# Head of an attention and feed-forward kernel: first loads re-dealt over three queues, q and half of v held until S1 lands, and PE filler matmuls laid differently

## The chip, the cores and the metric

The kernel runs on one core of a Trainium2 chip. Its metric is the time of one execution on the device in microseconds, the median of six runs. Five engines work side by side: PE (matrix products), DVE (VectorE), ACT (ScalarE), POOL (GpSimd) and SP (SyncE, which only issues transfers). Each runs its own list of instructions in order and meets the others through semaphores.

## The reference, cut to what matters

```python
batch, n_heads, seq, head_dim, r = 4, 4, 1088, 32, 8      # q, k, v: (4, 4, 1088, 32); S1, S2: (8, 32)

def phi(x):                       # polynomial sketch: 64 features from two 8-wide sketches
    a = np.einsum('rd,bhsd->bhsr', S1, x)
    b = np.einsum('rd,bhsd->bhsr', S2, x)
    return np.einsum('bhsi,bhsj->bhsij', a, b).reshape(*x.shape[:-1], r * r)
q_p, k_p = phi(q), phi(k)
kv = np.einsum('bhsf,bhsd->bhfd', k_p, v)
z = np.sum(k_p, axis=2)
attn = np.einsum('bhsf,bhfd->bhsd', q_p, kv) / (np.einsum('bhsf,bhf->bhs', q_p, z)[..., None] + 1e-06)
x = attn.transpose(0, 2, 1, 3).reshape(4352, 128)
h = x @ moe_w_in                  # (4352, 2048)
out = (h - np.tanh(h)) @ moe_w_out
```

## The kernel before

**Stages.** For each batch the kernel loads k, v and q with tokens on partitions, transposes k (`kT`), sketches it on PE (`ksk`), transposes the sketch back on DVE (`kab`), forms its outer products on DVE (`w`), and multiplies them with v on PE (`kvmm`, L740). The result is spread over a block pattern (`kvd` on ACT, `kvt` on PE, `kvb` on ACT). A Gram matrix of the k sketch (`gram`, L672; `gm`, L678; `scmm`, L682) gives the sum over tokens that the denominator needs. q is transposed (`qT`, L594), sketched, divided (`m`, `den`, `rd`, `ap`) and expanded (`qp`, `qpT`), and PE forms the attention output (L846), which ACT writes to `xT`. The feed-forward part runs over ten groups of 192 to 512 tokens: 16 products with w_in (L959), tanh on ACT (L964), 16 products with w_out (L974), a transposing copy on DVE (L983) and stores. h itself goes into the output through w_in times w_out, formed once on PE (L918, L930; `wch`, `wcl`).

**Order.** Nothing is written out in engine order. Each operation is added with what it reads and writes, a key, and an estimate of its time. `_Prog.schedule` then places operations one by one, the earliest that can start first, keys deciding among near ones, with an estimate for the landing of each load. `_Prog.sync` sets the semaphore waits. So an edit of an estimate can change an engine's order; on the chip each engine then runs its fixed list and waits for what really happens.

**The head, batch 0.** It is split finer than the other batches. k comes in two parts (`KPARTS`: blocks 0 to 3 and 4 to 8), each as two loads, one of 192 or 240 KB on SP and one of 64 or 48 KB on ACT. The two sketch matrices S1 and S2 go to `sq` as two loads of 16 KB; DVE transposes them (`stt`, L541) and forms `wab` (L549), the weights of the k sketch; POOL forms `s2r` (L559) and part of `wq3` (L544), the weights of the q sketch. The rest of `wq3` (`sc0`, L695) needs `scmm`. For the first two blocks of q, `q_tok` (L646) multiplies the transposed q with `wq3`, and the other seven blocks follow after `kvt`.

**Loads.** All go through `load` (L463), in the order of their keys, each on the queue of the engine given to it. Before, SP issues k's first big part, S1, k's second big part, q's first 128 KB, and two quarters of v; ACT issues S2, k's two small parts, the other two quarters of v, and the rest of q (416 KB). Then follow, on SP, four quarters of w_in (256 KB each), and on POOL two halves of w_out (`wo`). A limit on the bytes in flight (`IN_FLIGHT`) makes later loads wait for earlier ones. ACT casts w_in to bf16 as it comes (L912, eight casts `wi`).

**Fillers.** Where the planner sees PE idle for longer than a threshold and the first output bank isn't used yet, `fill` inserts matmuls of a zero tile `zz` (L426, 128x128x128 bf16), whose result nobody reads. Their number is fixed when the program is built. `WARM` is the time up to which the planner counts PE operations double.

Of the kernel before, what the change touches and what calls it, by code (L numbers as in the profile page):

```python
# [17 lines left out]

GCOLS = [256, 384, 448] + [512] * 6 + [192]
T_FIRST = 12500.0  # L20
KPARTS = [(0, 4), (4, 9)]
IN_FLIGHT = [4000000, 1600000, 1600000, 900000]
WIDE = 7
# [57 lines left out]

class _Op:
    __slots__ = ("engs", "fn", "key", "deps", "users", "nleft", "vals", "eng", "lat", "mode",
                 "t0", "t1", "seq", "known", "waits", "inc", "cnt", "sem", "dma", "name", "filler")


class _Prog:
    SWITCH = 95.0
    WARM = 9000.0

    def __init__(self):
        self.ops = []
# [2 lines left out]
    def add(self, engs, fn, r=(), w=(), key=0.0, chain=None, dma=0, name="", after=(), mode=None):  # L95
        o = _Op()
        o.engs = engs
        o.fn, o.key, o.dma, o.name, o.mode = fn, key, dma, name, mode
        o.deps, o.users, o.vals = {}, [], []
        o.filler = False  # L100
        tag = next(iter(o.engs)) if len(o.engs) == 1 and not dma else None
        for kind, vs in (("r", r), ("w", w)):
            for v in vs:
                if v not in o.vals:
                    o.vals.append(v)
                    v.left += 1
                ph = v.phases
                same = ph and ph[-1][0] == kind
                if same and v.psum and (tag is None or ph[-1][1] != tag):
                    same = False  # L110
                if not same:
                    ph.append((kind, tag, []))
                if len(ph) > 1:
                    raw = kind == "r" and ph[-2][0] == "w"
                    for d in ph[-2][2]:
                        o.deps[d] = o.deps.get(d, False) or raw
                if kind == "r":
                    for p in reversed(ph[:-1]):
                        if p[0] == "w":
                            for d in p[2]:  # L120
                                o.deps[d] = True
                            break
                ph[-1][2].append(o)
        for d in after:
            o.deps.setdefault(d, False)
        if chain is not None:
            o.deps.setdefault(chain, False)
        o.deps.pop(o, None)
        self.ops.append(o)
        return o  # L130

    def schedule(self, filler=None):
# [6 lines left out]
        free = {"tensor": 1100.0, "vector": 900.0, "scalar": 900.0, "gpsimd": 900.0, "sync": 800.0}  # L139
        self.order = {e: [] for e in free}  # L140
        dma_free = 0.0
# [21 lines left out]
        while n < len(self.ops):  # L163
            best = None
            for e in free:
                cands = []
                for o in ready:
                    if e in o.engs:
                        t = start_of(o, e)
# [4 lines left out]
                t0, f = min(cands, key=lambda x: (x[0], x[1].key))  # L174
# [6 lines left out]
            _, t, o, e = best  # L181
# [11 lines left out]
                    for d in v.first_deps:  # L193
                        o.deps.setdefault(d, False)
            if e == "tensor":
                if filler is not None and t - free[e] > 150.0 and not filler[2].used:
                    self.fill(filler, free[e], t)
                if pemode is not None and o.mode != pemode:
                    t += self.SWITCH
                pemode = o.mode  # L200
# [4 lines left out]
            if o.dma:  # L205
                free[e] = t + occ
                st = max(t + 1400.0, dma_free)
                dma_free = st + o.dma
                o.t1 = dma_free + (1200.0 if o.key < -95000 else 700.0 if o.key < -89950 else 1500.0)
            else:  # L210
                o.t1 = t + occ
                free[e] = o.t1
# [21 lines left out]
    def fill(self, filler, a, b):  # L234
        t = a
        while True:
            cold = 2.0 if t < self.WARM else 1.0
            occ = 54.0 * cold
            if t + occ + 60.0 > b:
                break  # L240
            o = _Op()
            o.engs = {"tensor": (occ, 215.0)}
            o.fn, o.key, o.dma, o.name, o.mode = filler[0], 0, 0, "fill", "128x128"
            o.deps, o.users, o.vals = {filler[1]: True}, [], []
            o.filler = True
            o.eng, o.t0, o.t1, o.lat = "tensor", t, t + occ, 215.0
            o.inc, o.sem, o.waits, o.known = False, None, [], {}
            o.seq = len(self.order["tensor"])
            self.order["tensor"].append(o)
            t = o.t1  # L250

    def sync(self, nc):
        known = {e: {} for e in self.order}
# [79 lines left out]
def bass_polysketch_attn__then__act_tanh_shrink_kernel(  # L333
# [74 lines left out]
    sq = sb("sq", [128, 2, 32])  # L408
# [46 lines left out]
    for b in range(B):  # L455
        P.add(_v(256), lambda e, n, b=b: e.memset(vL[b][96:128, :, 224:288], 0.0), w=[vvals[b][3]], key=-89000 + b)

    def load(key, o_, i_, w, nbytes, eng="sync", rate=320.0):
        need, j = nbytes, len(flight)
        while j > 0 and need + flight[j - 1][1] <= limit[0]:  # L460
            j -= 1
            need += flight[j][1]
        o = P.add({eng: (1100.0 if eng == "gpsimd" else 450.0, 0.0)}, lambda e, n: e.dma_start(out=o_, in_=i_), w=w, key=key, dma=nbytes / rate,  # L463
                  after=[f[0] for f in flight[:j]])
        flight.append((o, nbytes))
        return o

    flight, limit = [], [IN_FLIGHT[0]]

    def load_s(key, x, Sx, eng):  # L470
        load(key, sq[:, x, :], Sx[None, :, :].to_broadcast([16, 8, 32]), [sqv], 16384, eng)

    kpad = _Val(ap=kL[0][:, 1088:1152])
    pool_op(lambda e, n: e.memset(kpad.ap, 0.0), w=[kpad], n=64, key=-49500)
# [6 lines left out]
    def load_k(key, b):  # L481
        src = k[b].rearrange("h (t c) d -> (h t) (c d)", c=NC)
        if b == 0:
            kd = kL[b].rearrange("p (g x) -> p g x", g=4)
            ks = src[:, 0:864].rearrange("p (g x) -> p g x", g=3)
            for (lo, hi, kv_) in ((0, 128, kvals[b][0]), (128, 288, kvals[b][1])):
                load(key, kd[:, 0:3, lo:hi], ks[:, :, lo:hi], [kv_], 128 * 3 * (hi - lo) * 4, rate=290.0)
                load(key + 1, kd[:, 3, lo:min(hi, 224)], src[:, 864 + lo:864 + min(hi, 224)], [kv_],
                     128 * (min(hi, 224) - lo) * 4, "scalar", rate=290.0)
                key += 2  # L490
        else:
            load(key, kL[b][:, 0:576], src[:, 0:576], [kvals[b][0]], 128 * 576 * 4)
            load(key + 1, kL[b][:, 576:1088], src[:, 576:1088], [kvals[b][1]], 128 * 512 * 4)

    def load_v(key, b, eng="sync"):
        for g in (0, 2, 1, 3):
            w_ = (9 if g < 3 else 7) * 32
            vs = v[b].rearrange("h (t c) d -> t h (c d)", c=NC)[:, :, g * 288:g * 288 + w_]
            load(key + (0, 2, 1, 3)[g], vL[b][g * 32:(g + 1) * 32, :, 0:w_], vs, [vvals[b][g]], 128 * w_ * 4, "scalar" if b == 0 and g > 1 else eng, rate=205.0 if b else 300.0)

    def load_q(key, b, i, eng="sync"):
        a, z, val = qvals[b][i]
        src = q[b].rearrange("h (t c) d -> (h t) (c d)", c=NC)
        load(key, qL[b][:, a * 32:z * 32], src[:, a * 32:z * 32], [val], 128 * (z - a) * 128, eng, rate=330.0 if b else 250.0)

    wos = moe_w_out.rearrange("(jb ji) c -> ji jb c", jb=NJB, ji=128)

    lk = iter(range(-90000, -80000, 10))
    load_s(-99000, 1, S2, "scalar")
    load_k(next(lk), 0)  # L510
    load_s(-89999.5, 0, S1, "sync")
    load_q(next(lk), 0, 0)
    load_v(next(lk), 0)
    load_q(next(lk), 0, 1, "scalar")
    limit[0] = IN_FLIGHT[1]
    for i in range(4):
        load(next(lk), wif[i][:, :], moe_w_in[:, i * 512:(i + 1) * 512], [wifv[i]], 128 * 2048)
    for i in range(2):
        load(next(lk), woh[i].ap, wos[:, i * 8:(i + 1) * 8, :], [woh[i]], 128 * 4096, "gpsimd", rate=260.0)
    for b in range(1, B):  # L520
        limit[0] = IN_FLIGHT[2 if b == 1 else 3]
        load_k(next(lk), b)
# [45 lines left out]
    def nk():  # L568
        seq[0] += 1
        return -50000.0 + seq[0]  # L570
# [40 lines left out]
        P.add(_pe(540), sk, r=[kT[b], wab], w=[bk[0], bk[1]], key=nk(), mode="64x32", name=f"ksk{b}")  # L611
        back(b, bk, abk[b], 9, "kab")

    def k_part(i, banks):
        ab = abk[0]
        k0, k1 = KPARTS[i]
        n_ = k1 - k0

        def kg(a):
            return a.rearrange("p (g k t) -> p g k t", g=4, t=32)[:, :, k0:k1, :]  # L620
        P.add(_v(n_ * 128), lambda e, n: e.transpose(kg(kT0), kg(kL[0])),
              r=[kvals[0][i]] + ([kpad] if i else []), w=[kT0v[i]], key=nk(), name=f"kT0.{i}")

        def sk(e, n):
            for g in range(4):
# [250 lines left out]
    def attention_first():  # L876
        b = 0
        abc, abc2 = _Val(abc_p), _Val(abc_p)
        k_part(0, bk[0:2])
        k_outer(b, 0)  # L880
        gram(b, 0, 1)
        k_part(1, [_Val(bank_h), _Val(bank_h)])
        gram(b, 1, 2)
        q_transpose(b, 0)
        k_outer(b, 1)
        k_outer(b, 2)
        q_tok(b, 0, 2, abc, bk[1:2])
        q_transpose(b, 1)
        aq = q_divide(b, 0, 2, abc)
        kv_mm(b)  # L890
        kv_tail(b)
        q_tok(b, 2, 9, abc2, [_Val(bank_h), _Val(bank_h)], [P.kvt])
        q_piece(b, 0, 0, 2, abc, aq)
        aq = q_divide(b, 2, 9, abc2)
        for p in PIECES[b][1:]:
            q_piece(b, 2, *p, abc2, aq)
# [188 lines left out]
```

## Time and profile before

| what | value |
|---|---|
| median of six runs | 109.24 us (108.12, 108.82, 109.04, 109.43, 110.43, 110.60) |
| the profiled execution | 108.16 us, of which the span from the first to the last instruction is 106.0 us |
| PE busy | 96.8 us (91%) |
| ACT busy | 83.2 us (79%) |
| DVE busy | 67.8 us (64%) |
| fillers (L426) | 65, of them 57 before 16 us |
| first `wi` cast, first tanh | 10.85 us, 16.61 us |

Times in the profile count from the start of the span. Busy shares are means over stages with different limits, so a stage is read from its own waits. A wait is put down to what came last by the profile. In a row of the timeline stand start, length, engine, line, operation, what it writes and reads, how many instructions are merged, and in brackets the idle time before them and what ended it.

### The profile page before, as it was taken

What the parts mean: (1) busy time and instruction counts of PE and PEld (TensorE: products, weight loads), DVE (VectorE), ACT (ScalarE), POOL (GpSimd) and SP (SyncE); (2) the same over time, 40 slices, a digit from 0 to 9 for tenths busy, and PEclk for the clock granted to TensorE, in tenths of its full rate; (3) what the DMA queues carried; (4) which work ended last, traced back from release to release, by engine and by line L of the source; (5) the groups of instructions that cost most, each with busy time, mean ns of one, the idle gap of its engine ahead of it and who ended that gap; (6) DMA issues with size and microseconds to landing.
All of it is one profiled execution on the core that took longest, in us unless ns stands there. A gap on an engine that the chain in (4) does not pass through costs nothing.

```text
span 106.0 us, 3457 instructions
## 1 busy us (share of the span) xinstructions
PE 96.8 (91%) x1470; PEld 52.1 (49%) x1479; DVE 67.8 (64%) x114; ACT 83.2 (79%) x174; POOL 4.4 (4%) x22
## 2 busy tenths in 40 slices
PE   6947999999999999889999999999999999999960
PEld 6825897656654447343346453344444434334730
DVE  5399969987978999999999950999900020020210
ACT  0400699997488988487897987989999999999950
POOL 5110700000000000000000000000000000000000
PEclk9999999999999999999999999999999999999996
DMA  2999699959597396041000420051015024015054
GB/s 59 226 255 342 178 160 311 250 170 293 150 203 228 90 235 148 0 68 25 6 0 6 61 38 0 6 77 22 0 17 86 2 34 68 0 19 80 1 76 60
DMA packets 26542, 10.73 MB, mean 101 GB/s; under 512 B 21280, under 2 KB 24352, under 8 KB 26528
## 3 DMA queue, kind: packets, MB, share of 16 engines
q1 hardware_dynamic: 23168, 9.13, 36.9%
q0 software_dynamic: 2080, 0.52, 5.0%
q10 hardware_dynamic: 1280, 0.87, 3.5%
q8 instruction: 11, 0.18, 0.8%
q14 instruction: 3, 0.02, 0.1%
HBM read 8.81 MB, written 2.23 MB: 104 GB/s over the span
## 4 chain that ended last, share of the span: by engine, by line
PE 54%; ACT 28%; DVE 8%; DMA 4%; issue 2%; SPq 1%; DVEq 0%
ACT th L964 24%; PE pso L974 16%; PE psh L959 16%; PE psa L846 6%; DMA kL<-in_k_dram 4%; PE psa L740 3%; PE pso L978 2%; PE psa L725 2%; ACT xT L362 2%; PE psa L779 2%; ACT wi L912 1%; PE psa L608 1%; PE psa L672 1%; DVE w L710 1%; PE psh L846 1%
## 5 line engine op out<-in xcount | busy, mean ns | idle before, releaser
L964 ACT ACTIVATE th<-psh 128x512 bf16<-128x512 f32 (+4 forms) x115 | 63.6, 661 | 2.9 <-PE psh L959 2.4
L959 PE MATMUL psh<-xT,wi 128*128 128x512 bf16 (+4 forms) x140 | 43.6, 347 | 0.9 <-ACT xT L362 0.6
L974 PE MATMUL pso<-th,wo 128*128 128x512 bf16 (+3 forms) x123 | 39.3, 356 | 1.1 <-issue 0.6
L959 PEld LDWEIGHTS psh<-xT,wi 128*128 128x128 bf16 x143 | 13.4, 98 | 13.1 <-ACT th L964 1.9
L974 PEld LDWEIGHTS pso<-th,wo 128*128 128x128 bf16 x128 | 11.7, 97 | 15.2 <-ACT th L964 4.9
L983 DVE STREAM_TRANSPOSE ot<-pso 128x512 f32<-128x512 f32 (+3 forms) x8 | 5.3, 657 | 15.3 <-PE pso L974 15.2
L835 DVE STREAM_TRANSPOSE qpT<-qp 128x768 f32<-128x768 f32 (+1 forms) x14 | 12.1, 861 | 0.4
L710 DVE TENSOR_TENSOR w<-abk 128x768 f32<-128x768 f32 (+2 forms) x12 | 11.1, 951 | 0.2
L830 DVE TENSOR_TENSOR qp<-ap,abc 128x768 f32<-128x768 f32 (+1 forms) x13 | 10.7, 825 | 0.1
L846 PE MATMUL psa<-qpT,kvb 32*32 32x128 f32 (+4 forms) x336 | 8.3, 309 | 0.2
L846 PE MATMUL psh<-qpT,kvb 32*32 32x128 f32 (+4 forms) x112 | 8.3, 310 | 0.0
L964 ACT ACTIVATE th<-psa 128x1024 bf16<-128x1024 f32 (+2 forms) x9 | 8.3, 942 | 0.0
L974 PE MATMUL psa<-th,wo 128*128 128x512 bf16 (+1 forms) x32 | 7.5, 315 | 0.3 <-ACT th L964 0.2
L426 PE MATMUL pso<-zz 128*128 128x128 bf16 x65 | 6.5, 273 | 1.1 <-DVE zz L425 1.1
L846 PEld LDWEIGHTS psa<-qpT,kvb 32*32 32x32 f32 x336 | 5.2, 103 | 3.3 <-ACT th L964 1.3
L983 DVE STREAM_TRANSPOSE ot<-psa 128x512 f32<-128x512 f32 (+1 forms) x2 | 1.1, 550 | 8.7 <-PE psa L974 8.7
L426 PEld LDWEIGHTS pso<-zz 128*128 128x128 bf16 x65 | 5.6, 127 | 1.3 <-DVE zz L425 1.1
L594 DVE STREAM_TRANSPOSE qT<-qL 128x576 f32<-128x576 f32 (+3 forms) x8 | 5.7, 717 | 0.0
L959 PE MATMUL psa<-xT,wi 128*128 128x512 bf16 (+1 forms) x17 | 5.3, 348 | 0.0
L784 DVE STREAM_TRANSPOSE abc<-psh 128x288 f32<-128x288 f32 x3 | 1.4, 483 | 5.1 <-PE psh L779 5.1
L678 ACT ACT_TABLE_LOAD x1 | 1.3, 1283 | 4.1 <-issue 4.1
L678 ACT COPY gm<-psa 128x32 f32<-128x32 f32 x4 | 0.8, 198 | 4.5 <-PE psa L672 4.5
(86 smaller groups left out, 96.8 us busy)
## 6 DMA issues: line engine op xcount, KB each, us to landing
vL<-in_v_dram SPq DMA_DIRECT2D x11, 144.0 KB, 4.9
wif<-in_moe_w_in_dram SPq DMA_DIRECT2D x4, 256.0 KB, 4.6
out_dram<-ot SPq DMA_DIRECT2D x16, 64.0 KB, 2.0
kL<-in_k_dram SPq DMA_DIRECT2D x3, 288.0 KB, 3.9
qL<-in_q_dram SPq DMA_DIRECT2D x3, 288.0 KB, 3.5
kL<-in_k_dram SPq DMA_DIRECT2D x3, 256.0 KB, 4.6
qL<-in_q_dram SPq DMA_DIRECT2D x3, 256.0 KB, 3.1
wo<-in_moe_w_out_dram POOLq DMA_DIRECT2D x2, 256.0 KB, 5.1
```

Source lines behind the costliest of these rows:

```text
L362: return e.copy(o, i) if name == "scalar" else e.tensor_copy(o, i)
L426: filler = (lambda e, n: e.matmul(bank_o.slots[0][0][:, 0:128], zz.ap[:, 0:128], zz.ap[:, 128:256], start=True, stop=True), zop, bank_o)
L594: P.add(_v((z - a) * 32), lambda e, n: e.transpose(qTs[b][:, a * 32:z * 32], val.ap), r=[val], w=tvs, key=nk(), name=f"qT{b}.{i}")
L710: P.add(_v(nx * 64), lambda e, n: e.tensor_tensor(out=wv.ap[:, 0:nx * 64].rearrange("p (x i j) -> p x i j", i=8, j=8), in0=abh(0)[:, :, :, ...
L740: i = e.matmul(bk[2].ap[h * 32:(h + 1) * 32, 0:64], vL[b][:, h, blk * 32:(blk + 1) * 32], wvs[b, p].ap[:, (bi * 4 + h) * 64:(bi * 4 + h + ...
L830: P.add(_v(cn * 256), lambda e, n, qp=qp, c0=c0, cn=cn: e.tensor_tensor(out=qp.ap[:, 0:cn * 256].rearrange("p (x i j) -> p x i j", i=8, j= ...
L835: P.add(_v(cn * 256), lambda e, n, qp=qp, o0=o0, cn=cn: e.transpose(qt.ap[:, o0 * 256:(o0 + cn) * 256], qp.ap[:, 0:cn * 256]), r=[qp], w=[ ...
L846: i = e.matmul(banks[g].ap[h * 32:(h + 1) * 32, 0:nb * 32], kvb.ap[g * 32:(g + 1) * 32, x, h * 32:(h + 1) * 32], qq[g * 32:(g + 1) * 32, 0 ...
L959: return e.matmul(hv.bank(j // per)[:, c:c + n_], wib[:, jb * 128:(jb + 1) * 128], xt, start=True, stop=True)
L964: return e.activation(out=th.ap[:, 0:m * n_].rearrange("p (j x) -> p j x", x=n_), in_=i, func=AF.Tanh, scale=-1.0)
L974: fn = lambda e, n, x=x, st=st, sp_=sp_: e.matmul(ov.ap[:, 0:n_], wob[:, x, :], ths[x][0].ap[:, ths[x][1]:ths[x][1] + n_], start=st, stop=sp_)
L983: P.add(_vp(n_), lambda e, n: e.transpose(ot.ap[:, 0:n_], ov.ap[:, 0:n_]), r=[ov], w=[ot], key=-60000, name=f"ot{gi}")
```

## The change

- S1 becomes SP's first load, S2 POOL's first load, and all four k loads go to ACT, ahead of v and q there.
- q's first part and the two quarters of v that are on SP get an extra dependence on S1's load. SP issues in order, so everything after them on SP waits too.
- In `attention_first`, both k transposes come ahead in the recorded order, and q's pieces are recorded in another order.
- The planner gets given landing times for the head's loads (`land`) in place of rates. `WARM` goes from 9000 to 7900. `fill` plans fillers at half clock up to `COLD` = 13000, lets them reach past the planned start of the next operation up to `SOLID` = 7600, and hands back the time at which they end; the threshold for filling goes from 150 to 60 ns.

What the engines' lists become: DVE transposes q's first part after the second `kab` pair instead of ahead of the first. PE runs `q_tok` for the first two blocks ahead of all kv matmuls instead of after the first 16 of them, and has fillers in groups of 36, 8, 10, 3, 5, 2 up to `kvt` instead of 37, 1, 12, 3, 4. ACT casts the first quarter of w_in after `abc` instead of ahead of it. POOL issues S2 ahead of its memsets and forms `identb` last. DVE's four memsets of `vL` come ahead of the mask reductions. Further on, one neighbouring pair of PE's feed-forward matmuls is swapped; the rest of each list is the same.

```diff
+VLAND = [8600.0, 9900.0, 7600.0, 9200.0]
+QLAND = [6700.0, 10400.0]
...
 class _Prog:
     SWITCH = 95.0
-    WARM = 9000.0
+    OVER = 100.0
+    SOLID = 7600.0
+    WARM = 7900.0
+    COLD = 13000.0
...
-                if filler is not None and t - free[e] > 150.0 and not filler[2].used:
-                    self.fill(filler, free[e], t)
+                if filler is not None and t - free[e] > 60.0 and not filler[2].used:
+                    t = max(t, self.fill(filler, free[e], t))
...
     def fill(self, filler, a, b):
         t = a
         while True:
-            cold = 2.0 if t < self.WARM else 1.0
+            cold = 2.0 if t < self.COLD else 1.0
             occ = 54.0 * cold
-            if t + occ + 60.0 > b:
+            if t + occ + (60.0 if t > self.SOLID else -self.OVER) > b:
                 break
...
-                load(key, kd[:, 0:3, lo:hi], ks[:, :, lo:hi], [kv_], 128 * 3 * (hi - lo) * 4, rate=290.0)
+                load(key, kd[:, 0:3, lo:hi], ks[:, :, lo:hi], [kv_], 128 * 3 * (hi - lo) * 4, "scalar", land=l1)
...
-    load_s(-99000, 1, S2, "scalar")
+    s1 = load_s(-99000, 0, S1, "sync", 3600.0)
+    load_s(-98999, 1, S2, "gpsimd", 3900.0)
     load_k(next(lk), 0)
-    load_s(-89999.5, 0, S1, "sync")
-    load_q(next(lk), 0, 0)
-    load_v(next(lk), 0)
+    load_q(next(lk), 0, 0, "sync", [s1])
+    load_v(next(lk), 0, after=[s1])
     load_q(next(lk), 0, 1, "scalar")
...
     for i in range(4):
-        load(next(lk), wif[i][:, :], moe_w_in[:, i * 512:(i + 1) * 512], [wifv[i]], 128 * 2048)
+        load(next(lk), wif[i][:, :], moe_w_in[:, i * 512:(i + 1) * 512], [wifv[i]], 128 * 2048, land=10900.0 + 1000.0 * i)
...
         abc, abc2 = _Val(abc_p), _Val(abc_p)
+        k_part_t(0)
+        k_part_t(1)
         k_part(0, bk[0:2])
...
         q_tok(b, 0, 2, abc, bk[1:2])
-        q_transpose(b, 1)
         aq = q_divide(b, 0, 2, abc)
         kv_mm(b)
         kv_tail(b)
+        q_piece(b, 0, 0, 2, abc, aq)
+        q_transpose(b, 1)
         q_tok(b, 2, 9, abc2, [_Val(bank_h), _Val(bank_h)], [P.kvt])
-        q_piece(b, 0, 0, 2, abc, aq)
```

## The prediction

> **What bounds the kernel now.** I read the page first. The span is 106.0 us and the profiled execution took 108.16, so 2.16 us lie around the span. From the second slice on PE is busy almost all the time; the only soft places are the first three slices and the last two.
>
> ```profile
> span 106.0 us, 3457 instructions
> PE   6947999999999999889999999999999999999960
> DVE  5399969987978999999999950999900020020210
> ACT  0400699997488988487897987989999999999950
> ```
>
> After about 19 us the chain that ended last is nearly all PE and tanh, in an order that the change leaves alone but for one swapped pair of matmuls in the middle. So whatever the change moves in the head arrives at the end one for one, and the head must be read closely. This is the chain of waits in order of time (start, length, what):
>
> ```profile
> 1.96 4.08 DMA kL<-in_k_dram
> 6.14 0.84 DVE kT L621
> 6.98 0.42 DVE qT L594
> 7.41 0.41 DVE abk L632 x2
> 7.84 1.23 DVE w L710
> 9.06 0.50 DVE abk L632 x2
> 9.61 0.31 PE psa L672 x10
> ...
> 10.45 0.64 PE psa L740 x32
> 11.09 0.61 PE psa L646 x4
> 11.70 0.74 PE psa L740 x40
> 12.46 0.37 ACT kvd L362
> ...
> 13.74 0.61 ACT wi L912 x2
> 14.35 0.38 ACT abc L658
> ```
>
> The head waits 4.08 us for the second k part. Then VectorE sets the pace, then PE, then ScalarE. The timeline shows what else matters:
>
> ```profile
> 1.06 4.13 PE L426 MATMUL pso<-zz 128*128 128x128 bf16 x37 [1.06 <-DVE zz L425]
> 4.81 0.24 DVE L541 STREAM_TRANSPOSE stt<-sq 128x64 f32<-128x64 f32 x1 [1.81 <-DMA sq<-in_S_dram]
> 8.06 0.84 PE L426 MATMUL pso<-zz 128*128 128x128 bf16 x12
> 10.51 0.19 DVE L695 TENSOR_TENSOR wq<-psa,mask 128x32 f32<-128x32 f32 x1
> 10.66 2.00 POOL L463 DMA_DIRECT2D wo<-in_moe_w_out_dram x2 [4.90 <-DMA qL<-in_q_dram]
> ```
>
> The sketch `stt` waits for S1, which was issued second on SyncE at 1.25 and took 3.5 us. And the same filler matmul runs at two speeds: (4.13-0.31)/36 = 106 ns from one to the next in the first line, (0.84-0.22)/11 = 56 ns at 8.06. PE starts at half clock and had reached full clock by 8.06. Between the two, PE stood idle 0.78 us before 5.96 and again before 7.04, 7.86 and 9.61.
>
> **Part 1, the loads.** Landings are read from the trace's semaphore events. S2, first on ScalarE at 0.75, landed in 2.9 us (3.65); S1, now first on SyncE, should do the same: 3.65 instead of 4.7. S2 moves to POOL's queue, for which the trace has only wo: 1.06 us to issue and 4.8 from issue to landing, for 256 KB on busy queues. Bounds for the 16 KB of S2, issued near 0.7: the 2.9 of a small load (3.6) and wo's 4.8 (5.5). I take 3.9, because the queues are nearly empty then. `stt` starts 0.1 after: 4.0 instead of 4.81.
>
> POOL's memsets, `ident` and with them the three masks come up to 1.06 later, since the issue stands ahead of them. The last mask reduction ended at 2.33, so 3.4 now; they hide behind `stt` at 4.0, and were that cover gone each 0.1 us would delay `wab` by 0.1. `identb` goes last on POOL, near 5.3; its first use is past 11.9. ScalarE issues seven loads instead of six, some 0.6 us more before its table load (4.14); nothing wants ScalarE until `gm` near 8.8.
>
> All four k parts now stand in one queue with nothing ahead. The first took 2.7 us alone, so 3.5 for it and about 3.9 for its 64 KB partner: ahead of `kT0.0`, which starts at 4.4 (0.4 after `stt`, as before). The second part (240 and 48 KB) is issued near 1.9 and 2.5 as before, but competes with neither q nor v: lower bound 2.7 us, the uncontended first part (so 4.6 and 5.2); upper bound today's 4.1 (6.0). I take 5.2, nearer the uncontended row. `kT0.1` starts at 5.3 instead of 6.14.
>
> The price stands on SyncE: q's first part and two v parts wait there for S1, with the four w_in loads, and behind these all later k, v and q loads, queued after them. They are issued at 3.7 to 4.6 instead of 2.58 to 3.6, 1.05 us later. Lower bound nothing: the first q packets moved at 4.52 only, behind k, and the DMA share is 1.0 or more from 4 to 11 us, so the bytes find the same full engines; k simply goes first. Upper bound all 1.05: q's first part at 8.0 (wanted at 8.3), the last v at 11.1 instead of 10.05, w_in's third quarter at 14.4 instead of 13.36. I take +0.2 for each, nearer the lower end, since less stands ahead in both queues.
>
> [...]
>
> **Part 2, VectorE.** The transpose of q's first part moves behind the second `kab` pair. With the durations of the chain: `kT0.1` 5.30 to 6.14, `kab` to 6.57, the first w product to 7.79, `kab` to 8.34, qT to 8.76, the second product to 9.68, then `sc0` (`wq`, L695) at 9.68 instead of 10.51. That is 0.83 earlier. `gram`, `gm` and `scmm` follow `kab` at 8.34 and end near 9.2, so `sc0` doesn't wait for them.
>
> **Part 3, PE order.** q_tok now stands ahead of the first kv matmuls and waits for `sc0`; behind it on PE stand all the kv matmuls, the first w_in transposes and `kvt`, for which `kvd` and `kvb` on ScalarE wait. Before, 0.64 us of kv matmuls ran while `sc0` was still to come. That is given back: q_tok 9.9 to 10.52 (0.61), kv matmuls 0.64+0.74 to 11.90, `kvd` at 11.93 instead of 12.46. So 0.53 is left of 0.83. The last v has to land by 10.5 for this.
>
> **Part 4, ScalarE.** The first w_in casts move behind `abc`, into time in which ScalarE waited 0.51 us for the kv matmuls: nothing; without that wait they would cost their 0.61. The third pair of casts began at 13.64, right after `kvb`. `kvb` would allow 13.11, but the third quarter of w_in landed at 13.36. With +0.2 it would give back everything; if it takes the fourth's 4.0 us instead of its own 5.2 it is in by 12.5. Gain here between 0 and 0.53; I take 0.4, because a 5.2 us load is the exception among the four (median 4.6).
>
> **Part 5, fillers.** Seven more in sum (36, 8, 10, 3, 5, 2 instead of 37, 1, 12, 3, 4 before `kvt`). At 106 ns the 8 end at 6.4, when `kT0.1` is done; the 5 after `scmm` end near 9.75, before q_tok is allowed at 9.9. So they cost nothing, but the margin of the five is 0.15. What they may bring is seen in the times, not in this trace: the six runs spread over 2.5 us (108.12 to 110.60), and the profiled one is at their lower end. In it PE reached full clock in spite of the holes. If in others it stays at half clock up to `kvd`, the PE pieces from 9.61 to 12.46 (0.31+0.25+0.64+0.61+0.74 = 2.55) last up to twice as long: up to 2.5 us, which is the spread. After the change the holes before 8.1 are 0.2 to 0.3 us instead of up to 0.78. I take it that most runs then look like the profiled one.
>
> [...]
>
> **Sum.** 108.16 - 0.4 = 107.76 for a run like the profiled one. To the median I add 0.15 for what stays cold: the second `ksk` group (0.51) and the first `gram` (0.27) may run at half clock in some runs, mostly with slack. Forecast 107.9, against a median of 109.24.
>
> **Rivals.** (a) The clock isn't what spreads the runs (a late last DMA packet would do it as well). [...] Against it: nothing but PE changes its speed twofold here. Then the median falls by the head gain only: 109.24 - 0.4 = 108.8. (b) Slower: SyncE's hold. If the 1.05 us come through in full, w_in's third quarter lands at 14.4, its casts start near 14.5 instead of 13.64, and `abc` and the VectorE chain behind them follow: +0.9, with the spread left 110.1, and up to 110.6 if the last v (11.1) holds PE as well. It decides from a landing of that quarter past 13.55. For it: one queue in order, and the fourth quarter waits for the last v. Against it: q moved no byte before 4.52 today. (c) The change doesn't do what it says: S2 from POOL lands at 5.5, `stt` is later than now, `kT0.1` starts at 6.6, the moved qT gives back 0.42, `sc0` is at 10.95 and `kvd` at 13.2: +0.7, or 108.9 with a steady clock. Against it: wo's 4.8 is a large load on full queues.
>
> **Numbers.** Forecast 0.55, (a) 0.22, (b) 0.14, (c) 0.09. The forecast's own range is 107.2 to 108.5 (gain 0 to 0.8, remainder up to 0.35). Leaving out the far half of (b), and a rest below, the range is 107.0 to 109.7. A measurement of this kernel tells about 1% from no change, here 108.15 and 110.33. Faster: most of the forecast and a little of (a), 0.52. Slower: the far end of (b), 0.11. Same: 0.37.
>
> **What would show it.** Right: `stt` near 4.0, `kT0.1` near 5.3, `sc0` near 9.7, q_tok ahead of all kv matmuls, `kvd` near 11.9, the third casts before 13.4, and six times closer together than 2.5 us. Wrong: a spread as wide as before (a), SyncE's w_in landing later (b), `stt` after 4.8 (c), or a filler group still at 106 ns after 8 us.

## The result, and the profile after

The changed kernel takes 111.35 us (median of 22 runs, 109.76 to 113.68) against 109.13 us for the kernel before in the same sessions (46 runs, 108.0 to 111.6). The ratio is 1.0158, with a 95% interval of 1.0129 to 1.0188: slower by 1.6% (by the medians 2.0%); the prediction had 107.9 and a range up to 109.7. A ratio leaves out runs that lie more than 1.5% above the fastest of their kernel, while the medians below are over all runs, so that where a version spreads widely the two differ.

The profiled execution took 110.45 us, of which the span is 108.4. The page's head, in the rows that were shown of before, with the granted clock under them:

```profile
span 108.4 us, 3472 instructions
...
PE   6759899999999999979999999989999999999960
...
DVE  4657973996996999999999980699910020020210
ACT  0400259999638889669798996989999999999950
...
PEclk9995579999999999999999999999999999999997
```

DVE's third, fourth and seventh digits and ACT's fifth and sixth are lower than before, although nothing was taken from these engines in the head: they wait. The clock row has a dip in slices 4 to 6 (8 to 16 us) that the row of before does not have:

```profile
PEclk9999999999999999999999999999999999999996
```

The chain of waits of the changed kernel (start, length, what) says for what the engines wait:

```profile
0.74 2.83 DMA sq<-in_S_dram
...
3.58 6.68 DMA qL<-in_q_dram
...
10.29 0.45 DVE qT L605
...
11.73 1.17 PE psa L661 x4
12.90 2.04 PE psa L755 x72
...
14.96 0.37 ACT kvd L371
...
17.86 0.40 DVE m L819
```

Before, this chain began with k. Now it is S1, then the wait for S1 at which SyncE holds q, then q itself: 6.68 us from issue to landing where it took 4.4 before. `kvd` stands at 14.96 instead of 12.46 and `m` at 17.86 instead of 15.37. The 2.5 us lost up to `kvd` add up like this: `q_tok` (L661, before L646) starts at 11.73 instead of 11.09, +0.64; it takes 1.17 instead of 0.61, +0.56; behind it stand all 72 kv matmuls (2.04) instead of the last 40 (0.74), +1.30, of which 0.64 is the price of the 32 that no longer run ahead, and 0.66 is again a slower PE. The span ends 2.4 later, so the rest of the kernel neither adds nor gives back.

The timeline of the head (start, length, engine, line, operation, tiles, and in brackets the idle time before and what ended it):

```profile
4.22 0.24 DVE L552 STREAM_TRANSPOSE stt<-sq 128x64 f32<-128x64 f32 x1 [0.83 <-DMA sq<-in_S_dram]
...
5.40 0.45 PE L642 MATMUL psa<-kT,wab 64*32 64x128 f32 x16 [0.58 <-DVE kT L631]
...
6.63 0.84 DVE L631 STREAM_TRANSPOSE kT<-kL 128x640 f32<-128x640 f32 x1 [1.29 <-DMA kL<-in_k_dram]
...
7.53 0.59 PE L642 MATMUL psh<-kT,wab 64*32 64x160 f32 x16 [1.13 <-DVE kT L631]
...
8.32 1.25 PE L435 MATMUL pso<-zz 128*128 128x128 bf16 x10
...
10.29 0.45 DVE L605 STREAM_TRANSPOSE qT<-qL 128x256 f32<-128x256 f32 x1 [0.66 <-DMA qL<-in_q_dram]
```

`stt` did come forward (4.22 instead of 4.81), but the second k transpose went back (6.63 instead of 6.14), so PE stands idle 0.58 and 1.13 us where the fillers end too early, and VectorE waits 0.66 us for q. After these holes the ten fillers start 107 ns apart (nine of them from 8.40 to 9.26): half clock again. The granted clock by stretches (PE busy, PEld, DVE, ACT, POOL, clock, DMA share, GB/s):

```profile
4.42:7.83 3.41, 1.71 (x47) 1.05 (x44) 2.08 (x6) 1.10 (x1) 1.10 (x6) 1.00 0.99 248
7.90:14.60 6.70, 6.27 (x125) 5.07 (x120) 5.89 (x13) 1.01 (x4) 1.72 (x2) 0.50 0.78 201
```

PE had full clock from 4.42, lost it at 7.83 and had it back at 14.66. So two things are seen, late transfers and a slower PE, and the experiments had to tell which of them makes the time.

Landings in microseconds, from the trace's semaphore events of the profiled runs (the versions are explained below):

| version | k, second part (the later of its two loads) | q, first part | SyncE's v, last | w_in, last | bytes by 12 us as GB/s | profiled run |
|---|---|---|---|---|---|---|
| before | 6.04 | 6.94 | 10.05 | 14.06 | 221 | 108.16 |
| changed | 6.61 | 10.27 | 12.32 | 15.48 | 176 | 110.45 |
| e1, old loads | 6.20 | 6.88 | 9.79 | 14.49 | 225 | 108.15 |
| e2, new loads in before | 5.79 | 8.48 | 11.94 | 16.26 | 184 | 111.33 |
| e3, changed, no hold | 8.04 | 6.18 | 8.59 | 14.07 | 212 | 111.97 |
| j2, changed, v held only | 7.09 | 5.68 | 10.89 | 14.42 | 208 | 109.32 |
| d2, changed, more in flight | 6.07 | 8.57 | 11.52 | 14.24 | 212 | 109.40 |
| c2, changed, more fillers | 5.83 | 7.65 | 11.75 | 15.41 | 186 | 111.28 |
| d3, old loads and hold | 6.12 | 10.36 | 11.29 | 16.49 | 176 | 111.73 |
| j1, old loads, v held only | 6.75 | 7.48 | 11.95 | 15.01 | 186 | 110.19 |

The changed kernel, e2, c2 and d2 have the same head loads. q's landing varies among them (7.65 to 10.27); SyncE's last v is late in all four (11.52 to 12.32). In the eight profiles with before's loads and no hold, q landed at 6.52 to 7.14 and that v at 9.44 to 10.05. In these traces each of the head's loads shows sixteen landing events, and its landing is the last of them. Of q's, fifteen were in at 8.05 in the changed kernel and the last at 10.27 (in d3 8.87 and 10.36, before 6.57 and 6.94). Why one part stayed behind is not known.

### The profile page after: what moved, and what is told of

Read it like the earlier page. It is cut to its first block, busy times and chain, and to the rows that moved or that the text cites. A ratio compares the mean times of both kernels' runs of the same rounds, so it can differ in the third digit from the quotient of the medians.

```text
span 108.4 us, 3472 instructions
## 1 busy us (share of the span) xinstructions
PE 99.3 (92%) x1477; PEld 54.2 (50%) x1486; DVE 67.6 (62%) x114; ACT 83.0 (77%) x174; POOL 5.0 (5%) x23
## 4 chain that ended last, share of the span: by engine, by line
PE 53%; ACT 28%; DMA 9%; DVE 6%; issue 1%
ACT th L981 23%; PE pso L991 16%; PE psh L976 16%; DMA qL<-in_q_dram 6%; PE psa L861 6%; PE psa L755 3%; DMA sq<-in_S_dram 3%; PE pso L995 2%; PE psa L740 2%; ACT xT L371 2%; PE psa L794 2%; ACT wi L929 1%; PE psa L619 1%; PE psa L661 1%; DVE ot L1000 1%
## 5 line engine op out<-in xcount | busy, mean ns | idle before, releaser
L976 PEld LDWEIGHTS psh<-xT,wi 128*128 128x128 bf16 x143 | 13.4, 98 | 13.6 <-ACT th L981 2.0
L435 PE MATMUL pso<-zz 128*128 128x128 bf16 x72 | 7.7, 283 | 1.1 <-DVE zz L434 1.1
L435 PEld LDWEIGHTS pso<-zz 128*128 128x128 bf16 x72 | 6.4, 131 | 1.4 <-DVE zz L434 1.1
```

What stands on the lines that cost most here:

```text
L435: filler = (lambda e, n: e.matmul(bank_o.slots[0][0][:, 0:128], zz.ap[:, 0:128], zz.ap[:, 128:256], start=True, stop=True), zop, bank_o)
L976: return e.matmul(hv.bank(j // per)[:, c:c + n_], wib[:, jb * 128:(jb + 1) * 128], xt, start=True, stop=True)
```

## The experiments

In brackets stands each time the median of the kernel before in the same session.

### Loads or order: e1 and e2

e1 is the changed kernel with the loads dealt as before; e2 is the kernel before with the loads dealt as in the changed one, with the landing times that its planner had worked out before, so that the orders of PE, VectorE's work and ScalarE stay.

```diff
 e1:
-    s1 = load_s(-99000, 0, S1, "sync", 3600.0)
-    load_s(-98999, 1, S2, "gpsimd", 3900.0)
+    load_s(-99000, 1, S2, "scalar", 3900.0)
     load_k(next(lk), 0)
-    load_q(next(lk), 0, 0, "sync", [s1])
-    load_v(next(lk), 0, after=[s1])
+    load_s(-89999.5, 0, S1, "sync", 3600.0)
+    load_q(next(lk), 0, 0)
+    load_v(next(lk), 0)
 in load_k:
-    load(key, kd[:, 0:3, lo:hi], ..., "scalar", land=l1)
+    load(key, kd[:, 0:3, lo:hi], ..., land=l1)
 e2, on before: the lines marked - above in place of those marked +
```

> The changed kernel's order on PE, VectorE and ScalarE, with the same fillers, but the loads on their old queues and not held. Theory 1 (the loads cost it: q's first part landed at 10.27 us in the changed kernel's profile against 6.94 before, the last v at 12.32 against 10.05): near the kernel before, 108.6 to 109.6 us, with q's first part landing near 7 us and the first kv matmuls starting before 11.3. Theory 2 (the new order costs it, above all q_tok ahead of all kv matmuls and the fillers with the clock): near the changed kernel, 110.6 to 111.6.

> The kernel before, with its order on PE, VectorE and ScalarE and its fillers, but with the changed kernel's queues and hold. Theory 1 (loads): 110.8 to 112 us; in the old order q's transpose stands ahead of the kab pairs, so a q that lands at 10 us should even cost more than in the changed kernel. Theory 2 (order and fillers): 109.0 to 109.6.

Measured: e1 108.28 us (109.2; ratio 0.9939, 0.9903 to 0.9975), ten runs from 107.92 to 108.77. e2 111.32 (ratio 1.0209, 1.0118 to 1.0301). The loss comes with the loads, whatever the order; order and fillers alone cost nothing. In e2 VectorE waited for q up to 8.48, and q_tok and all kv matmuls ran at half clock (granted 0.50 from 9 to 15 us; q_tok took 1.17 us, before 0.61).

e1 was run once more, since the comparison leans on it:

> The version with the old loads and the new order and fillers once more, as it stands (e1_old_loads gave 108.28, ten runs within 0.9 us). The same version with before's fillers gave 110.17 and ran over 3.3 us. Theory (with the old loads the new fillers and order together do bring PE to full clock early in every run): 108.0 to 108.6 again, all runs within 1.2 us, ratio 0.99 to 0.997. Rival (the ten runs were lucky, or that chip was): a spread of 2 us or more and a median of 108.8 to 109.5.

d1 gave 108.93 (109.75; ratio 0.9982, 0.9938 to 1.0026), twelve runs, eleven of them from 108.1 to 110.67 and one of 112.46. The medians lie 0.9 and 0.8 below before in the two sessions, the second interval holds 1: with the old loads the new order and fillers are at best a little faster, and they don't make every run alike.

### The hold alone: d3 and c4, and what is held: j1 and j2

d3 is e1 with nothing but the hold (S1 stays second on SyncE, so q and v wait up to 4.54 instead of being issued at 2.59):

```diff
-    load_s(-89999.5, 0, S1, "sync", 3600.0)
-    load_q(next(lk), 0, 0)
-    load_v(next(lk), 0)
+    s1 = load_s(-89999.5, 0, S1, "sync", 3600.0)
+    load_q(next(lk), 0, 0, "sync", [s1])
+    load_v(next(lk), 0, after=[s1])
```

> The version with the old loads, with q's first part and SyncE's two quarters of v held until S1 has landed; S1 stays second on SyncE, so they are issued near 4.6 instead of 2.6: the hold alone, two us long, on the version that runs steadily. Theory (the hold costs what it delays, and more): q's first part lands 1.5 to 3 us later than 6.9, SyncE's last v past 11.3 instead of 9.8, w_in 1 to 2 us later; median 110 to 111, ratio 1.005 to 1.02. Rival (what costs is k in ScalarE's queue and S2 on GpSimd's): k's second part earlier by up to 0.5, q later by up to 0.7, median 108.0 to 108.8.

d3 took 111.79 (109.75; ratio 1.0261, 1.018 to 1.0343). Its chain of waits is that of the changed kernel:

```profile
1.25 3.28 DMA sq<-in_S_dram
...
4.54 5.81 DMA qL<-in_q_dram
...
10.38 0.45 DVE qT L605
...
11.82 0.81 PE psa L661 x4
12.63 2.08 PE psa L755 x72
```

An issue 1.95 us later became a landing 3.5 us later (10.36; 6.89 in d1); fifteen of its sixteen parts came 2.0 us later (8.87; 6.87), the last one made the rest. ScalarE's two v parts, which the hold does not touch, landed earlier (6.74 and 7.15; 7.49 and 8.56 in d1). PE was at full clock when q came late, stood idle 1.33 us before `q_tok`, and lost the clock at 12.24; the kv matmuls then took 2.08 us, 1.19 in d1. With the old loads the hold by itself makes a loss of the size of the change's: 111.79 against 108.93 for d1 in the same session.

c3 and c4 are the same pair with S1 first on SyncE, where the hold is short (q issued at 3.20 instead of 2.88):

```diff
 c3, on e1:
+    load_s(-98999, 0, S1, "sync", 3600.0)        # ahead of load_k
-    load_s(-89999.5, 0, S1, "sync", 3600.0)
 c4, on c3:
-    load_q(next(lk), 0, 0)
-    load_v(next(lk), 0)
+    load_q(next(lk), 0, 0, "sync", [s1])
+    load_v(next(lk), 0, after=[s1])
```

> The version with the old loads (108.28), with S1 moved ahead of k's first big part on SyncE; S2 first on ScalarE, as in before, and no hold. Theory (whatever goes first delays what follows by its own time on the queue only, and 16 KB are little): stt at 3.9 instead of 4.8, kT0.0 earlier or as before, k's second part and q up to 0.3 later; median 108.0 to 108.5. Rival (any change of who goes first lets q and v overtake k, as with S1 on POOL, where k's second part landed at 6.7): kT0.1 at 6.7, median 109.3.

> The same as c3_s1_first, with q's first part and SyncE's two quarters of v held until S1 has landed, as in the changed kernel: the hold alone. Theory (SyncE's hold is what costs most): q's first part lands 1 to 3 us later than in c3, SyncE's v 1 to 2 us, w_in 0.5 to 1.5; median 1.5 to 2.5 above c3, so 110 to 110.5. Rival (the hold costs little unless k stands in ScalarE's queue as well): q up to 0.5 later, median within 0.5 of c3.

c3 took 110.34 and c4 111.0 (109.29; c4's ratio 1.015, 1.0058 to 1.0241; c3's runs, 108.4 to 110.95, lie too far apart for one). From c3's profile to c4's q moved by 0.99 (7.84 to 8.83) for 0.32 us of hold, SyncE's last v by 0.65 and w_in's last quarter by 0.70; but k's second part, issued ahead of the hold, moved by 0.43 as well, so not all of this is the hold's. c3 itself contradicts what I expected of 16 KB put first: k's second part came at 6.96 (6.20 in e1) and PE fell to half clock from 8.39 to 15.22. With four runs of each, the 0.66 between the two is no proof; d3 is.

Which of the held loads matters? j1 is d3, j2 the changed kernel, each with q freed and only SyncE's v held.

```diff
-    load_q(next(lk), 0, 0, "sync", [s1])
+    load_q(next(lk), 0, 0)
```

> d3_old_loads_hold (111.79; q's first part landed at 10.36, SyncE's last v at 11.29, w_in's last quarter at 16.49) without the hold on q: SyncE's two quarters of v alone wait for S1. Theory (the time goes by q: VectorE waits for it, PE stands idle, and the late q also holds w_in's second quarter): q lands at 6.9 or earlier, w_in's last quarter by 14.8; v at 10.5 to 11.3 costs PE up to 0.7; median 109 to 110. Rival (the late v and w_in cost as much as q): median 111 or more.

> The changed kernel without the hold on q; SyncE's two quarters of v still wait for S1. Theory (as in j1): q lands near 6 to 6.5, its 128 KB ahead of k's second part make that up to 0.5 later (7.0), w_in's second quarter is issued near 7 instead of 10.3; median 109.5 to 110.6. Rival (k's second part, all in one queue, is then overtaken as in the kernel without any hold, where it landed at 8.0): kT0.1 at 7.5 or later, median 111 to 111.6.

j1 took 111.04 (109.81; ratio 1.0155, 1.0076 to 1.0234), although q landed at 7.48. I had expected 109 to 110. Holding v alone leaves 1.55% of loss of d3's 2.61% (the intervals overlap), so v and w_in weigh more than I had given them. Not all of it need be theirs: k's second part was late too (6.75), and PE was at half clock from 7.77 to 11.18. The chain of waits names v, and then w_out's first half, which the limit on bytes in flight lets go only when v has landed (issued at 12.56; before 10.66):

```profile
5.50 6.44 DMA vL<-in_v_dram
...
12.56 4.64 DMA wo<-in_moe_w_out_dram
```

j2 took 110.20 (ratio 1.0106, 1.0015 to 1.0197). By the ratios a third of the loss is gone without the hold on q, but the interval takes in the changed kernel's 1.0158, so this is not shown. k's second part landed at 7.09 (6.61 in the changed kernel).

### Through what it spreads: d2 and d4

In the changed kernel the second quarter of w_in could be issued only when q had landed (10.28; before 6.96), the third and fourth only when v had, by the limit on bytes in flight. d2 is the changed kernel, d4 is e1, with that limit lifted for these three quarters, which then wait for the first six loads alone (for w_out the limit is set again):

```diff
     for i in range(4):
-        load(next(lk), wif[i][:, :], ..., land=10900.0 + 1000.0 * i)
+        limit[0] = 3200000 if i else IN_FLIGHT[1]
+        load(next(lk), wif[i][:, :], ..., land=10900.0 + 1000.0 * i, after=[f[0] for f in flight[:6]] if i else ())
```

> The changed kernel with one thing different: the last three quarters of w_in don't wait for q's first part and SyncE's two quarters of v by the limit on bytes in flight; they are issued right after the first quarter, near 6.8 to 7.9 instead of 10.3 to 12.3. Theory (the late q and v hold w_in back through that limit, and w_in holds back w_out and batch 1's k, v and q, so that with full clock from 7 on the time stayed at 111.2): w_in lands 1 to 1.5 us earlier, the last quarter at 14.0 to 14.5 instead of 15.5, w_out's second half by 18.5, and the median is 110.0 to 110.6. Rival (the transfers move bytes at the same rate however many are issued, or PE's clock sets the time): w_in's last quarter at 15.0 or later, median 111.0 to 111.6.

> The version with the old loads, with the last three quarters of w_in issued right after the first, as in d2_more_in_flight. There the third quarter landed at 13.8 and set the end of the head by its casts. Theory (the limit on bytes in flight passes lateness on): the third quarter lands by 13.2, m is 0.3 to 0.6 earlier than 15.53, median 107.6 to 108.0. Rival (w_in then takes DMA time from v and q, or lands when it did): SyncE's last v past 10.3, median 108.3 to 109.

d2 took 110.12 (109.75; ratio 1.0075, 1.0012 to 1.0137): by the ratios half of the loss is gone, inside what was expected. w_in's last quarter landed at 14.24. What the profile still has is the late v itself:

```profile
4.49 7.02 DMA vL<-in_v_dram
...
11.56 1.26 PE psa L755 x72
```

d4 took 109.08 (ratio 1.0011, 0.9969 to 1.0054), no better than d1: where v is in time, the limit holds nothing back that counts, and the expected 107.6 to 108.0 did not come, although the third quarter landed at 12.01 and `m` began at 15.25.

### The clock: c2, c1, f2, b1, b2

c2 is the changed kernel with 41 and 22 fillers ahead of the two `ksk` groups instead of 36 and 8, to close the holes before 7.8 us. The fillers are given by number, ahead of the named PE operation:

```diff
+    COUNTS = {"ksk0.0": [41], "ksk0.1": [22], "gram0": [0, 10], "scmm0": [3], "qsk0.0": [5], "kvt0": [2], "h0.4": [8]}
```

> The changed kernel with 41 and 22 fillers ahead of the two ksk groups instead of 36 and 8, so that PE is busy where it stood idle from 4.83 to 5.40 and from 6.40 to 7.53; the loads are left as they are. Theory (half of the 2.5 us that kvd lost is clock: q_tok 0.56 and kv 0.66 longer, after a stretch in which PE was busy only half of the time): PE keeps full clock past 7.8, kvd is at 13.7 instead of 14.96, and the median is about 110.3. Rival (the landings alone decide; the clock goes its own way): half clock in the records from about 8 as before, median 111.3.

c2 took 111.19 (109.29; ratio 1.0172, 1.0089 to 1.0256), no better. But its profile had full clock from 6.96 on, and `kvd` at 13.08 instead of 14.96. The theory of the clock wanted 13.7; k and q also landed earlier in this profile (5.83 and 7.65), so the 1.9 us are not the clock's alone. They were lost again further on: the third `m`, the next batch's, starts at 36.41, against 36.07 in the changed kernel and 33.57 before.

```profile
11.80 1.21 PE L755 MATMUL psa<-w,vL 128*32 128x64 f32 x72 [0.75 <-DMA vL<-in_v_dram]
22.11 0.28 PE L991 MATMUL pso<-th,wo 128*128 128x256 bf16 x1 [0.31 <-DMA wo<-in_moe_w_out_dram]
25.22 0.78 DVE L605 STREAM_TRANSPOSE qT<-qL 128x576 f32<-128x576 f32 x1 [1.42 <-DMA qL<-in_q_dram]
34.27 0.78 DVE L605 STREAM_TRANSPOSE qT<-qL 128x576 f32<-128x576 f32 x1 [2.10 <-DMA qL<-in_q_dram]
```

PE waits for v (still ahead of `kvd`), then for w_out (its second half landed at 22.06; before 17.18), and VectorE waits 1.42 and 2.10 us for the q of later batches; before had none of these waits, and neither had the changed kernel for the later q. So with the engines earlier the late transfers cost as much. That the two hide each other, the slow clock making the engines late enough for the transfers to keep up, fits the changed kernel's profile and is argued from these two.

That the clock can cost as much, with the loads in time, is seen in c1: e1 with before's fillers.

```diff
+    COUNTS = {"ksk0.0": [37], "ksk0.1": [1], "gram0": [0, 12], "scmm0": [3], "qsk0.0": [0], "kvt0": [4], "h0.4": [8]}
```

> The version with the old loads and the new order and fillers gave 108.28 in ten runs that lay within 0.9 us, against 109.2 for before. Here it gets before's fillers back (37, 1, 12, 3, 4 up to kvt), nothing else. Theory (the new fillers made its runs alike, because PE's idle time ahead of 8 us goes to fillers): without them the runs spread over 2 us or more again and the median is 108.8 to 109.2. Rival (the order alone made the gain, by sc0 and q_tok): median 108.3, and the runs stay as close as before.

c1 took 110.17 (109.29; ratio 1.0039, 0.9982 to 1.0097), over 3.3 us. In its profiled run (111.98) PE stayed at half clock up to 17.06, with 224 GB/s by 12 us: its chain of waits has

```profile
12.52 2.08 PE psa L755 x72
```

where d1, at full clock, has 1.19 for the same matmuls. e1, with 225 GB/s and full clock from 5.23, took 108.15. The single runs go the same way. Of the 87 runs of before in the five sessions of experiments, 20 had a mean granted clock of 0.960 to 0.969 and took 109.34 to 111.45 us (median 110.49), and 48 had 0.983 to 0.996 and took 107.5 to 109.9 (median 108.98). Closer to 1 a mean tells less, because the time ahead of the first clock record counts as full: c1's profiled run, at half clock up to 17.06, has 0.997. So the runs spread with the clock, as the prediction had it, and the new fillers seem to help where the loads are in time: e1, d1 and d4 have medians 0.7 to 0.9 below before, c1 0.9 above (the intervals of c1's and d1's ratios overlap).

f2 gives before more fillers, and nothing else; b1 moves the transpose of q's first part behind the second `kab` pair in before; b2 moves `q_tok` ahead of all kv matmuls in before.

```diff
 f2, on before:
+    COUNTS = {"ksk0.0": [45], "ksk0.1": [5], "gram0": [3, 14], "scmm0": [3], "kvt0": [4], "h0.4": [8]}
 b1:
+    move('vector', 'qT0.0', 'kab0.1', True)      # after P.schedule
 b2:
+    move('tensor', 'qsk0.0', 'kvmm0.0', False)
```

> The kernel before with 45, 5, 3, 14, 3, 4 fillers in its PE gaps up to kvt instead of 37, 1, 0, 12, 3, 4, so that PE has no hole over 0.3 us up to 8 us in a run like the profiled one; all else as before. Theory of the forecast (the clock spreads the runs): the times draw together to about 1 us around 108.3. Rival (landings spread them): median 109.1 and a spread of over 2 us as before.

> The kernel before with one move: VectorE transposes q's first part after the second kab pair. Question: which part of the new order drew the times together in e1 (107.92 to 108.77, against 107.8 to 111.4 before). Theory Q (a late q holds VectorE in the old order): median 108.2 to 108.5, spread about 1 us. Theory T (PE's order does it): as before, 109.1, spread over 2 us.

> The kernel before with one move: q_tok ahead of all kv matmuls on PE. Theory Q: no better than before, 109.1 to 109.6, since 0.6 us of kv matmuls no longer hide in the wait for sc0. Theory T (a late v held up q_tok, and with it abc and the casts): median 108.3 to 108.6, spread about 1 us.

f2: 108.96 (109.2; ratio 0.9953, 0.9897 to 1.001), runs from 107.8 to 110.57, so longer fillers alone don't close the spread. b1: 108.59 (109.45; 1.0034, 0.9978 to 1.0091). b2: 110.62 by the median, 1.0026 (0.9972 to 1.0079) by the ratio; its runs fall into groups near 108.2 and 110.0 to 112.3, and the profiled one (111.57) was at half clock up to 17.18. Neither move costs or brings anything that can be measured beside that.

### The other load edits: e3, h1, g2

e3 is the changed kernel without the hold (`[s1]` and `after=[s1]` taken out); h1 is the changed kernel with k's big parts back on SyncE, behind S1, and the hold kept; g2 is e1 with S1 as GpSimd's first load.

```diff
 e3, on the changed kernel:
-    load_q(next(lk), 0, 0, "sync", [s1])
-    load_v(next(lk), 0, after=[s1])
+    load_q(next(lk), 0, 0, "sync")
+    load_v(next(lk), 0)
 h1, on the changed kernel, in load_k:
-    load(key, kd[:, 0:3, lo:hi], ..., "scalar", land=l1)
+    load(key, kd[:, 0:3, lo:hi], ..., land=l1)
 g2, on e1:
+    load_s(-98999, 0, S1, "gpsimd", 3900.0)      # ahead of load_k
-    load_s(-89999.5, 0, S1, "sync", 3600.0)
```

> The changed kernel without the two dependences on S1's load: SyncE issues q's first part and its two v quarters at once after S1; k still alone in front on ScalarE's queue, S2 on POOL's. Theory 1a (the hold is what costs): q lands near 7.5 us, the last v near 10.5, time 109.0 to 109.8. Theory 1b (the dealing of the queues costs, k, half of v and most of q all on ScalarE): 110.3 to 111.3. Theory 2: as the changed kernel, 111.3.

> The changed kernel with k's two big parts back on SyncE, right behind S1; the hold of q and of SyncE's two v quarters, and S2 on POOL, stay. e2 and the changed kernel show that the loads cost it (+2.2 us), e3 that leaving out the hold doesn't help while k is all on ScalarE's queue. Theory 1 (k, half of v and most of q behind one another on ScalarE is the harm; the hold alone is small): 108.3 to 109.3 us, the second k part landing near 5.5, q near 8. Theory 2 (the hold starves SyncE's queue, whoever carries k): q after 8 us, the last v after 11.5, w_in after 12, and 110 to 111.5 us.

> e1 (new order, old loads, no hold) with one part of the new loads: S1 goes to POOL's queue, S2 stays first on ScalarE's, k stays on both, so that SyncE issues k's second big part 0.7 us earlier. Theory A (VectorE is gated by k's second part, landed at 6.2 in e1): it lands near 5.5, the kT0.1 transpose starts near 5.6, the time falls by 0.3 to 0.6 us below e1's 108.28, to 107.7 to 108.0. Theory B (the landing of w_in's third quarter and its casts set the head's end): same as e1, 108.2 to 108.5.

e3 took 111.51 (109.2; ratio 1.0256, 1.0183 to 1.0329), h1 111.61 (109.45; 1.0299, 1.021 to 1.0387), g2 109.33 (109.45; 1.0105, 1.004 to 1.017). Taking the hold away does not repair the changed kernel, since q and v from SyncE then land early (6.18 and 8.59) and the second part of k, which stands in ScalarE's queue alone, late:

```profile
2.24 5.80 DMA kL<-in_k_dram
```

Here k's second part lands at 8.04 (before 6.04), in h1 at 6.92, in g2 at 6.73. Each edit put one load first, and the next one was late. The old deal, with S1 between the two halves of k and k on both queues, is the one in which k, q, v and w_in each come shortly before they are wanted; no version was measurably faster than it except e1 in its first session.

## Why the prediction was wrong

**Part 1, the hold (the step that failed).** The text took +0.2 us for q, v and w_in, and at most the 1.05 us by which they are issued later. Measured against before: q +3.33, SyncE's last v +2.27, w_in's quarters +1.91, +2.04, +1.50 and +1.42. The upper bound was no bound. It took for granted that a transfer issued 1.05 later lands at most 1.05 later. In the four profiles with the changed head loads SyncE's last v was issued 0.82 to 0.91 us later than before and landed 1.47 to 2.27 later; q was issued 0.94 to 1.03 later and landed 0.71 to 3.33 later, the most where one of its parts stayed behind. In d3 ScalarE's v, issued meanwhile, came earlier; whether that is the whole cause of the delay stays open. And the limit on bytes in flight, which the section on the loads names, turned the landing of q and v into the issue of w_in; the prediction looked at the third quarter, and not at what each quarter waits for. That the hold costs is shown with the old loads (d3). In the changed kernel it can't be taken out by itself: without it k is late (e3). The argument "q moved no byte before 4.52 anyway" was about the first byte, where the last one counts.

**Part 1, k.** 5.2 was taken for the second part, 6.0 as the upper end; it landed at 6.36 and 6.61. "Competes with neither q nor v" was wrong: ScalarE's own two v loads are issued right behind it. By the trace's packet records their first packet moved at 4.19, and the last bytes of k's 240 KB were through at 5.35, no earlier than before (5.33); its semaphore event came another 1.0 us later (0.7 before). In e2, c2 and d2, with the same head loads, the second part landed at 5.79 to 6.07, so a k as late as 6.61 is not in every run. `kT0.1` started at 6.63 (5.3 predicted). S1 at 3.56 (3.65) and S2 at 4.20 (3.9, bounds 3.6 to 5.5) were right, and `stt` at 4.22 (4.0) with them: the gain was where it was expected, on a wait that was not the last.

**Parts 2 and 3.** With k and q late, `sc0` came at 11.49 (9.68) and `kvd` at 14.96 (11.93). The order's own price was right: the 0.64 us of kv matmuls given back is in the sum above, and b1, b2 and e1 show no cost of the order. The condition "the last v has to land by 10.5" was written down; it landed at 12.32.

**Part 4.** The third casts began at 16.13 (13.4 at the latest).

**Part 5.** The mechanism stands: the spread goes with the clock (c1 and b2, half clock up to 17; before's profile at full clock from 5.35; the 87 runs), and little is left of rival (a), though a late transfer can be what opens the hole in PE's work (in d3 q landed at 10.36, PE stood idle 1.33 us before `q_tok`, and the clock fell at 12.24). But the fillers were counted by the planner's landing times, so the holes were 0.58 and 1.13 us, not 0.2 to 0.3, and the clock, once there, was lost again.

**The deal of the queues.** It brought no bytes: up to 12 us the changed kernel moved 176 GB/s, and e3, without the hold, 212 (before 221). e3, h1 and g2, three other deals of the first loads, took 111.51, 111.61 and 109.33 us; none was faster than before, and by the ratios (1.0256, 1.0299, 1.0105) each cost time.

**Rivals.** (b), slower by the hold, at 0.14, was right in its place and its test (a third quarter past 13.55: 14.86; the last v past 11.1: 12.32), and its 110.1 to 110.6 was 1 us short: its delay was capped at the issue's, and PE's clock was left out. (c), S2 late, did not happen.

## What to carry to other kernels

A wait put ahead of a transfer is not priced by the time that it waits: here v landed 1.5 to 2.3 us later for an issue 0.8 to 0.9 later, and a limit on bytes in flight handed the delay on, to w_in, w_out and the next batches. Before moving a load, write down for each later one which landing its issue waits for. And where two things are late together, curing one may move no time (c2); take each away by itself, in a version where the other is in order (d3, c1).

## What the hardware showed that was not expected

**Busy transfer engines that move less.** The stretch from 2 to 12 us of before (columns as above):

```profile
2.00:12.00 10.00, 7.74 (x166) 6.15 (x167) 7.74 (x18) 2.39 (x5) 2.44 (x8) 1.00 0.96 263
```

The same stretch of e2 has a DMA share of 0.95 and 219 GB/s: as busy, 17% fewer bytes. By the packet records of the changed kernel, w_in's packets of 2048 bytes took 112 ns on the mean (96 before) and q's of 1024 bytes 88 ns (55). Which transfers side by side cause this was not tried. Among the profiled runs at full clock from 7 us or earlier, the time follows the bytes moved by 12 us: 221 to 229 GB/s with 107.88 to 108.73 us (before, e1, d4, f2), 208 and 212 with 109.32 and 109.40 (j2, d2), 186 with 111.28 (c2).

**The granted clock changed 3.41 us or twice that apart, and it fell with PE about half busy or less.** In the changed kernel it was full from 4.42 to 7.83 and half to 14.66 (3.41 and 6.83), in d3 full from 5.42 to 12.24 and half to 15.65 (6.82 and 3.41), in j1 full from 4.36 to 7.77 and half to 11.18 (3.41 twice). Eight of the twenty profiles lost full clock like this in the head (the changed kernel, b1, c3, c4, d3, e2, h1, j1). In the changed kernel's stretch from 4.42 to 7.83 PE was busy 1.71 us of 3.41 (its row stands in the section on the result); these are b1's stretch, after which the clock was half, and one of before, which kept full clock (columns as above):

```profile
4.42:7.83 3.41, 1.85 (x52) 1.05 (x50) 2.71 (x7) 1.00 (x1) 0.92 (x4) 1.00 1.09 267
```

```profile
5.35:8.76 3.41, 2.02 (x53) 1.30 (x53) 3.15 (x6) 0.07 (x1) 0.41 (x3) 1.00 1.07 256
```

From 5 to 8 us PE was busy 1.30 us of 3 in e2 and 1.00 of 3 in c4, and from 9 us both had a granted clock of 0.50. What share of busy PE keeps the clock was not tried by itself. Nor did the clock come back after one busy stretch in the changed kernel: it stayed at half with PE busy 3.30 of 3.41 us (7.83 to 11.24) and 3.10 of the next 3.42, and was full from 14.66.

**What a late clock costs.** c1 and e1, with the same loads in time, took 111.98 and 108.15 in their profiled runs: 3.8 us, 3.5% of the time, with a clock that came at 17.06 instead of 5.23 (c1's k landed 0.39 us later, so a part of it is not the clock's).
